# First-batch q and k rows over all partitions, halves swapped in the cast, and a block of unread products moved ahead of the first channel mix

## The chip, the cores and the metric

The kernel runs on one core of a Trainium2 chip. The metric is the device time of one execution in microseconds (us); lower is better. A core has TensorE (PE, matrix products), VectorE (DVE), ScalarE (ACT), GpSimd (POOL) and SyncE (SP), which here only issues transfers. Times of before are from three runs and one profiled execution.

## What is computed

Eight batches of 576 tokens with 8 heads of 64 channels go through block-causal attention (blocks of 64 tokens, each block sees itself and the earlier ones); the result, 512 channels per token, goes through a channel mix with a hidden width of 1024. All inputs and the output are float32 in DRAM.

```python
scores = scale * np.matmul(q, k.transpose(0, 1, 3, 2))
scores = np.where(block_i >= block_j, scores, -1000000000.0)
attn = softmax(scores)                    # over the keys
x = np.matmul(attn, v)                    # heads side by side: (B, S, 512)
x_prev = x shifted by one token, zero ahead of the first
xk = mu_k * x + (1.0 - mu_k) * x_prev
xr = mu_r * x + (1.0 - mu_r) * x_prev
k = np.maximum(xk @ w_k, 0.0)             # 512 -> 1024
v = k * k @ w_v                           # 1024 -> 512
r = 1.0 / (1.0 + np.exp(-(xr @ w_r)))     # 512 -> 512
return r * v
```

## The kernel before

**Order.** All work is registered as tasks with an engine, a planned duration, a rank, what it depends on, and the buffers it takes from rings. `Plan.order` walks a planned clock and at each moment gives each engine the ready task of lowest rank; the program is then written in that order, so every engine's queue has a fixed order and only semaphores decide the real times. The ranks stand in a table `RANK`, most of it for the first batch (`loads`, `qkt0`, `score0`, `av0`, `xt0`, `mix0`, `pk0`, `pr0`, `pv0`), and a few offsets (`qk`, `v`, `qkt`, `av`, `xt`, `mix`, `xr`, `moe`) that hold for every later batch. So a change of a rank or of a planned duration can move instructions anywhere in the program. All loads and stores are issued by SP, in one queue.

**Attention of one batch.** q and k are loaded, cast to bf16 (`t_nb`), transposed on PE by a product with an identity, and copied out of PSUM to `t_qkt` (channels on partitions). Scores (`t_s`, L509) are exponentiated on ACT to `t_e` (L530; three pieces for a pair of heads, and one further piece `EL` for the last 64 keys of all heads), POOL zeroes the masked corners (L538). Then come the products with v (`t_mm` in batch 0, `t_m` later, L567; 15 for a head, with a column of ones for the sum), a reciprocal and a multiplication on DVE (L584, L585, output `t_x`), and a transpose back (L637) that ACT copies to `t_xt` (L616). `t_e` has three buffers for four pairs of heads, `t_s` two.

**The first batch's q and k** are loaded differently from the others: a tile holds 4 heads (a group, g = 0 or 1), and each partition holds nine consecutive tokens of a head, which are 2304 contiguous bytes. The tile is [128, 2, 576] and uses the rings of `t_xk` (q) and `t_xr` (k), which the channel mix needs only later. One transfer fills 64 partitions with two heads, a second the other 64. Two casts, one for each of the tile's two columns of heads, write `t_nb`, and `add_long_qkt` transposes it in nine blocks of 128x128: eight of q, eight of k, and the ninth of both together.

**The channel mix** works on chunks of 512 tokens, nine in all. For each 128 channels, POOL or DVE subtracts the shifted tokens (`t_d`, L675), DVE makes `t_xk` and `t_xr` (L687). `add_pk` multiplies with WK (L723, 4 products of 128x512 for each of eight parts), ACT takes the relu to `t_kr` (L733) and DVE squares it (L739). `add_pr` multiplies with WR (L752) and ACT takes a tanh; `add_pv` multiplies with WV (L775) and DVE joins the two to `t_o`, which SP stores. The results of pk, pr and pv, of batch 0's products with v, and of the unread products below share two PSUM buffers (`mm`). The weights come as 20 loads into the ring `ld` of ten buffers and are cast to fp16, WK by POOL, WR and WV by ACT.

**Unread products.** `warm` multiplies an identity with itself, four products of 128x128 at a time, into an `mm` buffer that nobody reads. It depends on nothing and has the highest ranks (1000 and up), so the plan puts the 18 tasks (72 products) wherever PE has nothing else at the start: 48 before the first transposes, 12 after q's, 12 after k's.

Of the kernel before, what the change touches and what calls it, by code (L numbers as in the profile page):

```python
# [13 lines left out]
ALU = mybir.AluOpType  # L14


WARM = 18

RANK = {
# [18 lines left out]
 'qkt': -5.5,  # L40
 'av': 3.0,
 'xt': 5.5,
 'mix': 41.5,
 'xr': 114.5,
 'moe': 17.5,
}


# [90 lines left out]
def kernel(  # L139
# [13 lines left out]
    B, H, S, D = q.shape  # L153
# [17 lines left out]
    plan = Plan(RINGS)  # L171
# [10 lines left out]
    def new(ring, shape, dtype):  # L182
        return pools[ring].tile(shape, dtype, tag=ring, name="t_" + ring)
# [26 lines left out]
    def step(b, n=0):  # L210
        return b * NP_ + n

    tiles = {}


    def load(dst_key, make, jobs, rank, dur, deps=(), takes=(), uses=()):
        def fn():
            if make is not None:
                tiles[dst_key] = make()
            for dst, src in jobs(tiles[dst_key]):  # L220
                nc.sync.dma_start(dst, src)  # L221
# [34 lines left out]

    JT = S // D

    LONG = {(0, 0): ("DVE", "POOL"), (0, 1): ("POOL", "ACT"),
            (1, 0): ("POOL", "DVE"), (1, 1): ("POOL", "DVE")}  # L260

    def add_long(g, ranks):


        for n, src in enumerate((q, k)):
            ring = ("xk", "xr")[n]
            ld, nb = plan.buf(ring), plan.buf("nb")
            tiles["nbbuf", 0, g, n] = nb
            key = ("ld", 0, g, n)
            t = load(key, lambda ring=ring: new(ring, [P, 2, S], FP),  # L270
                     lambda d, src=src: [
                         (d[y * D:y * D + D], src[
                             0, 4 * g + 2 * y:4 * g + 2 * y + 2].rearrange(
                                 "x (p j) d -> p x (j d)", j=JT))
                         for y in range(2)], ranks[n], 1.8, takes=[ld])
            cast["qk", 0, g, n] = []
            for x in range(2):
                def fn(n=n, key=key, x=x):
                    if x == 0:
                        tiles["nb", 0, g, n] = new("nb", [P, JT, P], BF)  # L280
                    dst = tiles["nb", 0, g, n][:, :, x * D:x * D + D]
                    src = tiles[key][:, x].rearrange("p (j d) -> p j d", d=D)
                    eng = LONG[g, n][x]
                    if eng == "ACT":
                        nc.scalar.copy(dst, src)
                    elif eng == "DVE":
                        nc.vector.tensor_copy(dst, src)
                    else:
                        nc.gpsimd.tensor_copy(dst, src)
                cast["qk", 0, g, n].append(on(  # L290
                    LONG[g, n][x],
                    {"ACT": 0.7, "DVE": 0.5, "POOL": 0.78}[LONG[g, n][x]],
                    ranks[n], fn, [t], takes=[] if x else [nb],
                    uses=[ld] + ([nb] if x else [])))

    def add_tail(b, rank):
        tl, tb = plan.buf("tl"), plan.buf("tb")
# [55 lines left out]
    evac = {}  # L353
# [311 lines left out]
    def add_mix(c, cc, rank):  # L665
        d = plan.buf("d")
        if cc == 0:
            tiles["xkb", c], tiles["xrb", c] = plan.buf("xk"), plan.buf("xr")
            mixed[c, 0], mixed[c, 1] = [], []
        eng = "DVE" if cc % 2 else "POOL"  # L670

        def fn():
            tiles["d", c, cc] = new("d", [P, CH], FP)
            x = tiles["xt", c]
            (nc.vector if eng == "DVE" else nc.gpsimd).tensor_tensor(  # L675
                tiles["d", c, cc], x[:, cc, 1:CH + 1], x[:, cc, 0:CH],
                ALU.subtract)
        sub = on(eng, 0.8 if eng == "DVE" else 1.3, rank, fn,
                 list(xt_of[c][cc]), takes=[d], uses=[xtbuf[c]])
        for n in range(2):  # L680
            name = ("xk", "xr")[n]
            buf = tiles[name + "b", c]

            def mul(n=n, name=name):
                if cc == 0:
                    tiles[name, c] = new(name, [P, CCn, CH], F16)
                nc.vector.scalar_tensor_tensor(  # L687
                    tiles[name, c][:, cc], tiles["d", c, cc],
                    (MUK1, MUR1)[n][:, cc:cc + 1],
                    tiles["xt", c][:, cc, 1:CH + 1], ALU.mult, ALU.add)  # L690
# [116 lines left out]
    R = RANK  # L807


    wbuf = plan.buf("mm")  # L810

    def warm(i):
        if i == 0:
            tiles["warm"] = new("mm", [P, CH], FP)
        for x in range(4):
            nc.tensor.matmul(tiles["warm"][:, x * P:(x + 1) * P], identb,
                             identb, start=True, stop=True)
    for i in range(WARM):
        on("PE", 0.43, 1000 + i, lambda i=i: warm(i), [],
           takes=[] if i else [wbuf], uses=[wbuf] if i else [])  # L820

    at = {x: -99 + i for i, x in enumerate(R["loads"])}
    t = on("SP", 0.6, at["mu"], mus, [])
    mu_ready.append(on("DVE", 0.3, at["mu"], mu1, [t]))
    for b in range(B):
        r = step(b)
        if b == 0:
            for g in range(2):
                add_long(g, [at[f"g{g}q"], at[f"g{g}k"]])
# [82 lines left out]
```

## Time and profile before

| | |
|---|---|
| median of 3 runs | 294.98 us (294.54 to 295.31) |
| the profiled execution | 294.23 us, span of its instructions 292.1 us |
| PE busy | 271.1 us, 93% of the span |
| DVE, ACT, POOL busy | 76%, 64%, 46% |
| DMA | 43.44 MB; most loads have pieces of 256 bytes |
| granted PE clock, mean over the span | 0.959 |

The profile page gives busy times, 40 equal slices of the span (7.3 us each) with the busy tenths of each engine and the PE clock granted, the chain of work that ended last, and groups of instructions by line. Other views of the same trace: the chain in order of time, a timeline of instructions with the idle time ahead of each and what ended it ("[2.75 <-DMA t_xk]"), and tables of busy times in stretches that one chooses. "SPq" is SP issuing a transfer. A count ("x10") joins instructions of one kind that follow each other.

### The profile page before, as it was taken

The numbers are of one execution on the slowest core, as the hardware profiler recorded it, in microseconds if no ns is written. First come the engines' busy times: TensorE is split into PE (matmuls) and PEld (weight loads), VectorE is DVE, ScalarE is ACT, GpSimd is POOL, SyncE is SP. The second block draws the span as 40 slices with busy tenths as digits, with TensorE's granted clock in tenths as the row PEclk, the third lists the DMA queues.
The fourth block names the chain that finished last, engine by engine and source line by source line (L and its number), as shares of the span: only waits on it lengthen the run. The fifth ranks groups of instructions, "written<-read, shape, count | busy, mean of one in ns | idle before, by whom it ended". The sixth has DMA issues, their size and how long they took to land.

```text
span 292.1 us, 6893 instructions
## 1 busy us (share of the span) xinstructions
PE 271.1 (93%) x2584; PEld 154.8 (53%) x2584; DVE 221.4 (76%) x394; ACT 187.1 (64%) x295; POOL 134.8 (46%) x283
## 2 busy tenths in 40 slices
PE   7658669999799999999999999999999999999995
PEld 7425425566465545664655655565556555544442
DVE  3453896459979686998599779977986797898541
ACT  0587935867669548864886588657866795361530
POOL 2256763667868573956395618371512123301000
PEclk9676959999899999999999999999999999999999
DMA  7999999489999999939996895111001101201102
GB/s 163 260 204 322 323 202 210 121 189 218 212 198 216 212 244 209 244 78 209 274 204 130 218 237 116 38 45 66 2 36 41 73 1 39 108 0 74 72 36 108
DMA packets 114337, 43.44 MB, mean 149 GB/s; under 512 B 106112, under 2 KB 106112, under 8 KB 114304
## 3 DMA queue, kind: packets, MB, share of 16 engines
q1 hardware_dynamic: 114304, 43.01, 62.3%
q8 instruction: 20, 0.33, 0.5%
q14 instruction: 13, 0.11, 0.1%
HBM read 33.56 MB, written 9.44 MB: 147 GB/s over the span
## 4 chain that ended last, share of the span: by engine, by line
PE 82%; DVE 8%; DMA 5%; ACT 1%; SPq 1%; issue 1%; POOL 1%; DVEq 0%; POOLq 0%
PE t_mm L775 22%; PE t_mm L723 21%; PE t_mm L752 10%; PE t_m L567 9%; PE t_s L509 8%; PE t_m L637 6%; PE t_m L370 5%; DMA t_xk<-in_q_dram 2%; DMA t_xr<-in_k_dram 2%; PE t_mm L567 1%; DVE t_k L739 1%; SPq L221 1%; DVE t_xk L687 1%; DVE t_x L585 1%; DVE t_d L675 1%
## 5 line engine op out<-in xcount | busy, mean ns | idle before, releaser
L530 ACT ACTIVATE t_e<-t_s 128x1024 f16<-128x1024 f32 x96 | 95.3, 1024 | 26.7 <-PE t_s L509 23.6
L723 PE MATMUL t_mm<-t_xk,WK 128*128 128x512 f16 x288 | 72.7, 391 | 4.9 <-DVE t_xk L687 4.1
L775 PE MATMUL t_mm<-WV,t_k 128*128 128x512 f16 x288 | 66.8, 379 | 0.7 <-ACT t_t L762 0.7
L739 DVE TENSOR_TENSOR t_k<-t_kr 128x512 f16<-128x512 f32 x72 | 56.7, 797 | 10.8 <-ACT t_kr L733 10.6
L538 POOL MEMSET t_e<- 64x128 f16 x128 | 23.7, 200 | 77.6 <-ACT t_e L530 74.1
L733 ACT ACTIVATE t_kr<-t_mm 128x512 f32<-128x512 f32 x72 | 43.1, 599 | 21.2 <-PE t_mm L723 20.8
L775 PEld LDWEIGHTS <-t_k 128*128 128x128 f16 x288 | 27.5, 98 | 33.3 <-issue 2.7
L248 POOL CAST t_nb<-t_ld 128x512 bf16<-128x512 f32 x56 | 42.7, 779 | 4.0 <-DMA t_ld<-in_q_dram 1.6
L723 PEld LDWEIGHTS <-WK 128*128 128x128 f16 x288 | 27.1, 100 | 32.3 <-issue 9.0
L785 DVE SCALAR_TENSOR_TENSOR t_o<-t_t,t_mm 128x512 f32<-128x512 f32 x36 | 24.7, 685 | 20.8 <-PE t_mm L775 13.6
L567 PEld LDWEIGHTS <-t_e 128*128 128x128 f16 x896 | 34.3, 99 | 9.7 <-PE t_s L509 2.7
L509 PE MATMUL t_s<-t_qkt 64*128 64x64 bf16 (+4 forms) x384 | 34.3, 288 | 4.2 <-DVE t_qkt L446 2.2
L616 ACT COPY t_xt<-t_m 128x256 f32<-128x256 f32 (+7 forms) x68 | 24.0, 394 | 20.4 <-PE t_m L637 20.4
L752 PE MATMUL t_mm<-WR,t_xr 128*128 128x512 f16 x144 | 36.8, 382 | 0.0
L567 PE MATMUL t_m<-VO,t_e 128*128 128x65 f16 x784 | 32.9, 195 | 0.4 <-DVE t_qkt L389 0.2
L762 ACT ACTIVATE t_t<-t_mm 128x512 f32<-128x512 f32 x36 | 21.6, 600 | 17.0 <-PE t_mm L752 16.3
L687 DVE SCALAR_TENSOR_TENSOR t_xk<-t_d,MUK,t_xt 128x512 f16<-128x512 f32 x36 | 30.1, 844 | 0.3
L675 POOL TENSOR_TENSOR t_d<-t_xt 128x512 f32<-128x512 f32 x18 | 21.3, 1182 | 19.7 <-ACT t_xt L616 9.4
L687 DVE SCALAR_TENSOR_TENSOR t_xr<-t_d,MUR,t_xt 128x512 f16<-128x512 f32 x36 | 29.7, 836 | 0.0
L322 POOL CAST VO<-t_vl 128x512 f16<-128x512 f32 (+1 forms) x40 | 28.4, 728 | 2.1 <-DMA t_vl<-in_v_dram 0.9
L585 DVE TENSOR_TENSOR t_x<-t_m,t_r 128x320 f32<-128x320 f32 x56 | 27.5, 491 | 1.9
L509 PEld LDWEIGHTS <-t_qkt 64*128 64x128 bf16 x384 | 12.8, 96 | 25.5 <-issue 17.5
(54 smaller groups left out, 239.5 us busy)
## 6 DMA issues: line engine op xcount, KB each, us to landing
out_dram<-t_o SPq DMA_DIRECT2D x36, 256.0 KB, 2.1
t_vl<-in_v_dram SPq DMA_DIRECT2D x32, 256.0 KB, 5.0
t_ld<-in_q_dram SPq DMA_DIRECT2D x56, 128.0 KB, 3.6
t_ld<-in_k_dram SPq DMA_DIRECT2D x56, 128.0 KB, 3.4
t_ld<-in_moe_w_k_dram SPq DMA_DIRECT2D x8, 256.0 KB, 5.3
t_ld<-in_moe_w_v_dram SPq DMA_DIRECT2D x8, 256.0 KB, 5.8
t_xk<-in_q_dram SPq DMA_DIRECT2D x4, 288.0 KB, 5.4
t_xr<-in_k_dram SPq DMA_DIRECT2D x4, 288.0 KB, 5.6
```

The lines of the kernel that those rows point to most:

```text
L248: nc.gpsimd.tensor_copy(tiles["nb", b, pr][:, n], tiles[key][:, :].rearrange("p t h d -> p t (h d)"))
L322: nc.gpsimd.tensor_copy(VOs[b % 2][0:n, sc, :, 0:D], tiles["vl", b, sc][0:n])
L509: nc.tensor.matmul(PS[:, h, col:col + n], qkt[rows, pr, 1, kc * P:kc * P + P], qkt[rows, pr, 0, q0:q0 + n], start=True, stop=True)
L530: nc.scalar.activation(tiles["e", b, pr][:, :, i, :], tiles["ps", b, it], AF.Exp, scale=ISQ)
L567: nc.tensor.matmul(PA[:, mt * D1:(mt + 1) * D1], stationary(b, h, kc, mt), VOs[b % 2][:, kc, h, 0:D1], start=(kc == 0), stop=(kc == mt))
L585: nc.vector.tensor_tensor(tiles["x", b, pr][:, :, h % 2 * D:(h % 2 + 1) * D], view[:, :, 0:D], Rc[:, :].unsqueeze(2).to_broadcast([P, 5, D ...
L687: nc.vector.scalar_tensor_tensor(tiles[name, c][:, cc], tiles["d", c, cc], (MUK1, MUR1)[n][:, cc:cc + 1], tiles["xt", c][:, cc, 1:CH + 1], ...
L723: nc.tensor.matmul(ps, WK[:, cc, jc * P:(jc + 1) * P], tiles["xk", c][:, cc], start=(cc == 0), stop=(cc == CCn - 1))
L733: nc.scalar.activation(tiles["kr", c, jc], tiles["pk", c, jc], AF.Relu)
L739: nc.vector.tensor_tensor(tiles["k2", c][:, jc], KR, KR, ALU.mult)
L752: nc.tensor.matmul(ps, tiles["xr", c][:, cc, jt * P:(jt + 1) * P], WR[:, cc], start=(cc == 0), stop=(cc == CCn - 1))
L775: nc.tensor.matmul(ps, tiles["k2", c][:, jc, jt * P:(jt + 1) * P], WV[:, jc], start=(jc == 0), stop=(jc == JCn - 1))
```

## The change

The first batch's q and k transfers each cover all 128 partitions: the two heads of one transfer are contiguous in DRAM, and go to partitions 0-63 and 64-127 of one column of the tile. The heads therefore sit at other places than before, and the cast puts them right: of its four pieces (64 partitions x 576 elements each), two stay in their half of the partitions and two move to the other half. There are 16 casts where there were 8, distributed over DVE, ACT and POOL by the table `LONG`. The unread products are no longer free to stand at the start: they depend on the normalised results of all eight heads of batch 0 and have rank -5, there are twelve tasks (48 products) instead of 18 (72), and their planned time is lower. All ranks are new.

```diff
-WARM = 18
+WARM = 12
...
- 'loads': ['g0q', 'g0k', 'g1q', 'wk6', 'wv2', 'wv5', 'v4', 'mu', 'wv4',
...
+ 'loads': ['g0q', 'g0k', 'g1k', 'g1q', 'wk7', 'v0', 'wk2', 'v4', 'v2',
...
- 'qk': [-30.5, -24.0, -13.0, -12.5],
+ 'qk': [-17.0, -15.0, -11.5, -14.5],
...
-    LONG = {(0, 0): ("DVE", "POOL"), (0, 1): ("POOL", "ACT"),
-            (1, 0): ("POOL", "DVE"), (1, 1): ("POOL", "DVE")}
+    LONG = {(0, 0): ("DVE", "POOL", "DVE", "ACT"),
+            (0, 1): ("ACT", "POOL", "DVE", "ACT"),
+            (1, 0): ("POOL", "DVE", "DVE", "POOL"),
+            (1, 1): ("POOL", "DVE", "DVE", "POOL")}
...
-                         (d[y * D:y * D + D], src[
-                             0, 4 * g + 2 * y:4 * g + 2 * y + 2].rearrange(
-                                 "x (p j) d -> p x (j d)", j=JT))
-                         for y in range(2)], ranks[n], 1.8, takes=[ld])
+                         (d[:, x], src[0, 4 * g + 2 * x:4 * g + 2 * x + 2]
+                          .rearrange("y (p j) d -> (y p) (j d)", j=JT))
+                         for x in range(2)], ranks[n], 1.8, takes=[ld])
...
-            for x in range(2):
+            for i, (x, y) in enumerate(((0, 0), (1, 1), (1, 0), (0, 1))):
+                eng = LONG[g, n][i]
...
-                    dst = tiles["nb", 0, g, n][:, :, x * D:x * D + D]
-                    src = tiles[key][:, x].rearrange("p (j d) -> p j d", d=D)
+                    dst = tiles["nb", 0, g, n][
+                        x * D:x * D + D, :, y * D:y * D + D]
+                    src = tiles[key][y * D:y * D + D, x].rearrange(
+                        "p (j d) -> p j d", d=D)
...
-                    {"ACT": 0.7, "DVE": 0.5, "POOL": 0.78}[LONG[g, n][x]],
+                    eng, {"ACT": 0.7, "DVE": 0.5, "POOL": 0.68}[eng],
...
-    for i in range(WARM):
-        on("PE", 0.43, 1000 + i, lambda i=i: warm(i), [],
-           takes=[] if i else [wbuf], uses=[wbuf] if i else [])
...
+    wbuf = plan.buf("mm")
+    for i in range(WARM):
+        on("PE", 0.3, -5, lambda i=i: warm(i),
+           [evac["x", 0, h] for h in range(H)],
+           takes=[] if i else [wbuf], uses=[wbuf] if i else [])
```

SP's queue at the start of the program; each row is a transfer's tile, source and shape. Before:

```order
L221 DMA t_xk<-in_q_dram 64x2x576 x2
L221 DMA t_xr<-in_k_dram 64x2x576 x2
L221 DMA t_xk<-in_q_dram 64x2x576 x2
L221 DMA t_ld<-in_moe_w_k_dram 128x512
L221 DMA t_ld<-in_moe_w_v_dram 128x512 x2
L221 DMA t_vl<-in_v_dram 64x8x64
L799 DMA MUK<-in_moe_mu_k_dram 128x4x1
L800 DMA MUR<-in_moe_mu_r_dram 128x4x1
L221 DMA t_ld<-in_moe_w_v_dram 128x512
L221 DMA t_xr<-in_k_dram 64x2x576 x2
L221 DMA t_vl<-in_v_dram 128x8x64 x4
```

Now:

```order
L221 DMA t_xk<-in_q_dram 128x576 x2
L221 DMA t_xr<-in_k_dram 128x576 x4
L221 DMA t_xk<-in_q_dram 128x576 x2
L221 DMA t_ld<-in_moe_w_k_dram 128x512
L221 DMA t_vl<-in_v_dram 128x8x64
L221 DMA t_ld<-in_moe_w_k_dram 128x512
L221 DMA t_vl<-in_v_dram 64x8x64
L221 DMA t_vl<-in_v_dram 128x8x64 x2
L221 DMA t_ld<-in_moe_w_k_dram 128x512
L221 DMA t_vl<-in_v_dram 128x8x64
```

The second group's k, which stood behind three weights of WV, one of WK, a part of v and the two mu, now stands third, and the second group's q fourth; v comes between single weights.

DVE's queue from its first cast on (L444 and L446, now L450 and L452, copy transposed blocks to `t_qkt`). Before:

```order
L287 CAST t_nb<-t_xk 128x9x64
L434 MEMSET t_qkt 128x4x32
L444 COPY t_qkt<-t_m 128x2x64x8
L446 COPY t_qkt<-t_m 128x4x64
L287 CAST t_nb<-t_xk 128x9x64
L444 COPY t_qkt<-t_m 128x2x64x8
L803 TENSOR_SCALAR MUK_139<-MUK 128x4
L804 TENSOR_SCALAR MUR_140<-MUR 128x4
L287 CAST t_nb<-t_xr 128x9x64
L444 COPY t_qkt<-t_m 128x2x64x8
L446 COPY t_qkt<-t_m 128x4x64
```

Now:

```order
L294 CAST t_nb<-t_xk 64x9x64 x2
L440 MEMSET t_qkt 128x4x32
L450 COPY t_qkt<-t_m 128x2x64x8
L294 CAST t_nb<-t_xr 64x9x64 x3
L452 COPY t_qkt<-t_m 128x4x64
L294 CAST t_nb<-t_xk 64x9x64 x2
L450 COPY t_qkt<-t_m 128x2x64x8 x2
L452 COPY t_qkt<-t_m 128x4x64
```

DVE has seven casts where it had three; one cast of the first group's k stands behind the copy of q, and two of the second group's k stand ahead of the copy that the first scores need.

ACT's queue from batch 0's last exponentials to the first relu (WV and WR are casts of weights). Before:

```order
L530 ACTIVATE t_e<-t_s 128x2x512 x6
L344 CAST WR<-t_ld 128x512
L616 COPY t_xt<-t_m 128x512 x2
L347 ACTIVATE WV<-t_ld 128x512 x2
L344 CAST WR<-t_ld 128x512
L347 ACTIVATE WV<-t_ld 128x512
L616 COPY t_xt<-t_m 128x512 x2
L344 CAST WR<-t_ld 128x512 x2
L347 ACTIVATE WV<-t_ld 128x512
L616 COPY t_xt<-t_m 128x4x64
L347 ACTIVATE WV<-t_ld 128x512
L733 ACTIVATE t_kr<-t_mm 128x512 x3
```

Now:

```order
L536 ACTIVATE t_e<-t_s 128x2x512 x2
L622 COPY t_xt<-t_m 128x512 x2
L353 ACTIVATE WV<-t_ld 128x512 x4
L350 CAST WR<-t_ld 128x512
L622 COPY t_xt<-t_m 128x512
L622 COPY t_xt<-t_m 128x4x64
L353 ACTIVATE WV<-t_ld 128x512
L350 CAST WR<-t_ld 128x512 x2
L353 ACTIVATE WV<-t_ld 128x512
L350 CAST WR<-t_ld 128x512
L353 ACTIVATE WV<-t_ld 128x512
L739 ACTIVATE t_kr<-t_mm 128x512 x7
```

More of the casts of WV and WR stand behind the last copies of `t_xt`: six between the copy of 4x64 and the first relu, where there was one.

On PE the 72 unread products at the start are gone; 48 stand between the last transposes of batch 0's results (L643) and the first product with WK (L729). On DVE, `t_xk` and `t_xr` of the first 128 channels now stand ahead of the normalisation of the last two heads, not behind it. For the later batches, the new offsets let SP load a batch's q and k in one stretch and later in the order than before, when the first pair of heads was loaded up to two batches ahead.

More of the change, by code (lines that the diff above doesn't have):

```diff
@@ L14 @@
 ALU = mybir.AluOpType
-WARM = 18
+WARM = 12
 RANK = {
[18 rows of a table removed]
- 'qkt': -5.5,
[L41 to L45, printed above, removed]
[18 rows of a table added]
+ 'qkt': -5.5,
+ 'av': 3.5,
+ 'xt': 6.0,
+ 'mix': 26.0,
+ 'xr': 52.5,
+ 'moe': 18.0,
 }
@@ L271, in add_long, with fn @@
                      lambda d, src=src: [
-                         (d[y * D:y * D + D], src[
-                             0, 4 * g + 2 * y:4 * g + 2 * y + 2].rearrange(
-                                 "x (p j) d -> p x (j d)", j=JT))
-                         for y in range(2)], ranks[n], 1.8, takes=[ld])
+                         (d[:, x], src[0, 4 * g + 2 * x:4 * g + 2 * x + 2]
+                          .rearrange("y (p j) d -> (y p) (j d)", j=JT))
+                         for x in range(2)], ranks[n], 1.8, takes=[ld])
             cast["qk", 0, g, n] = []
-            for x in range(2):
-                def fn(n=n, key=key, x=x):
-                    if x == 0:
+            for i, (x, y) in enumerate(((0, 0), (1, 1), (1, 0), (0, 1))):
+                eng = LONG[g, n][i]
+                def fn(n=n, key=key, x=x, y=y, i=i, eng=eng):
+                    if i == 0:
                         tiles["nb", 0, g, n] = new("nb", [P, JT, P], BF)
-                    dst = tiles["nb", 0, g, n][:, :, x * D:x * D + D]
-                    src = tiles[key][:, x].rearrange("p (j d) -> p j d", d=D)
-                    eng = LONG[g, n][x]
+                    dst = tiles["nb", 0, g, n][
+                        x * D:x * D + D, :, y * D:y * D + D]
+                    src = tiles[key][y * D:y * D + D, x].rearrange(
+                        "p (j d) -> p j d", d=D)
                     if eng == "ACT":
@@ L290, in add_long @@
                 cast["qk", 0, g, n].append(on(
-                    LONG[g, n][x],
-                    {"ACT": 0.7, "DVE": 0.5, "POOL": 0.78}[LONG[g, n][x]],
-                    ranks[n], fn, [t], takes=[] if x else [nb],
-                    uses=[ld] + ([nb] if x else [])))
+                    eng, {"ACT": 0.7, "DVE": 0.5, "POOL": 0.68}[eng],
+                    ranks[n], fn, [t], takes=[] if i else [nb],
+                    uses=[ld] + ([nb] if i else [])))
     def add_tail(b, rank):
@@ L807 @@
     R = RANK
-    wbuf = plan.buf("mm")
     def warm(i):
```

32 rows, old and new, of the table RANK are left out of this document.

## The prediction

> **What bounds the kernel now.** I read the page's busy times and slices first, then a table of stretches, then the chain in order of time for the start. In the stretch rows the columns are PE, PE's weight loads, DVE, ACT and POOL busy, the granted PE clock, DMA share and GB/s.
>
> ```profile
> span 292.1 us, 6893 instructions
> PE 271.1 (93%) x2584; PEld 154.8 (53%) x2584; DVE 221.4 (76%) x394; ACT 187.1 (64%) x295; POOL 134.8 (46%) x283
> ```
>
> ```profile
> 27.00:29.00 2.00, 2.00 (x40) 1.51 (x39) 1.19 (x5) 1.97 (x3) 1.49 (x4) 0.97 1.05 399
> 30.00:40.00 10.00, 4.76 (x55) 3.08 (x51) 9.71 (x17) 7.11 (x14) 7.50 (x10) 0.87 1.05 266
> 70.00:80.00 10.00, 7.76 (x91) 4.78 (x90) 9.68 (x18) 7.60 (x13) 8.86 (x19) 0.92 1.10 213
> 100.00:150.00 50.00, 49.28 (x504) 28.26 (x502) 39.93 (x74) 35.88 (x59) 30.56 (x62) 1.00 0.91 205
> ```
>
> From about 40 us on PE is the bound (49.28 of 50 us busy), except between 70 and 80, where DVE is (9.68 of 10). Before 40 us PE waits, and in the last ten of these DVE carries the work (9.71). So a microsecond saved ahead of the first dense stretch of products is worth a microsecond at the end, as long as 70 to 80 doesn't take it back. The chain shows what the start consists of:
>
> ```profile
> 4.13 7.22 DMA t_xk<-in_q_dram
> 12.01 6.03 DMA t_xr<-in_k_dram
> 18.13 0.77 DVE t_nb L287
> ...
> 22.47 0.59 ACT EL L518
> ...
> 24.63 1.76 PE t_mm L567 x30
> ...
> 39.33 4.42 PE t_mm L723 x10
> 43.75 1.14 PE t_mm L752 x4
> 44.88 1.73 PE t_mm L723 x8
> ```
>
> Two loads of the second group in a row lead to its cast at 18.13; dense work begins at 39.33, its first ten products at 442 ns, the later eight at 216.
>
> **The loads.** The start in order of time (start, length, engine, line, what ended the idle time before):
>
> ```profile
> 0.75 1.39 SPq L221 DMA_DIRECT2D t_xk<-in_q_dram  x2
> 6.05 0.75 DVE L287 CAST t_nb<-t_xk 128x576 bf16<-128x576 f32 x1 [2.75 <-DMA t_xk<-in_q_dram]
> 6.08 0.66 POOL L289 CAST t_nb<-t_xk 128x576 bf16<-128x576 f32 x1 [4.25 <-DMA t_xk<-in_q_dram]
> 7.59 1.23 DVE L444 COPY t_qkt<-t_m 128x1024 bf16<-128x1024 bf16 x1 [0.65 <-PE t_m L421]
> 8.74 1.28 ACT L285 ACT_TABLE_LOAD   x1 [8.74 <-DMA t_xr<-in_k_dram]
> 10.03 0.67 ACT L285 CAST t_nb<-t_xr 128x576 bf16<-128x576 f32 x1
> 10.85 1.23 PE L421 MATMUL t_m<-identb,t_nb 128*128 128x128 bf16 x10 [2.62 <-ACT t_nb L285]
> 12.11 1.29 DVE L446 COPY t_qkt<-t_m 128x256 bf16<-128x256 bf16 x1 [3.29 <-PE t_m L421]
> 13.04 0.95 DVE L287 CAST t_nb<-t_xk 128x576 bf16<-128x576 f32 x1
> 14.20 1.94 ACT L530 ACTIVATE t_e<-t_s 128x1024 f16<-128x1024 f32 x2 [0.76 <-PE t_s L509]
> 20.82 1.26 DVE L446 COPY t_qkt<-t_m 128x256 bf16<-128x256 bf16 x1
> ```
>
> q is in at 6.05 and k at 8.74: 1.35 us for a transfer of 288 KB, 219 GB/s. Counted back, data begin to land at 3.35. The trace has no such row for 128 partitions. The bounds are 1.35 (no gain) and 0.74 (the 399 GB/s of 27 to 29 us, where weights of 128 rows of 2 KB arrive). I take 0.80, near the second, since the shape is almost that one. SP needs 0.70 for an issue, so it stays ahead. Then q's two transfers land at 4.15 and 4.95, k at 6.55, the second k at 8.15, the second q at 9.75.
>
> **The casts.** Sixteen for eight, and 64 partitions instead of 128 shorten nothing if the time goes by the 576 elements of a partition: I keep 0.75 on DVE, 0.66 on POOL, 0.67 on ACT. The ends are half of these and, for a cast that moves between halves or runs beside POOL's, DVE's slower one of 0.95. ACT's table load, which here waits for k, stands in the new order ahead of all waits and is hidden by the wait for q; with that cover gone it costs 1.28. q: DVE 4.15 to 4.90 and 4.95 to 5.70, POOL to 5.61, ACT to 4.82; eight transposes at 123 ns (the ten in 1.23) to 6.7; DVE's copy to 8.0; DVE's piece of k to 8.75; ten transposes to 10.0. Meanwhile two DVE casts of the second k, to 10.25, then the copy that the first scores need, 1.29: 11.55. Before, that copy ended at 13.40 and ACT began 0.80 later, so the first exponential moves from 14.20 to 12.35: 1.85 earlier. The second group: two casts (1.5), three copies (1.23, 1.23, 1.26), 16.8, against 22.08. Five exponentials at 0.97 from 12.35 last to 17.2, so ACT no longer waits for the second group.
>
> **To the last normalisation.**
>
> ```profile
> 27.03 2.85 ACT L530 ACTIVATE t_e<-t_s 128x1024 f16<-128x1024 f32 x3 [1.25 <-POOL t_e L538]
> 29.05 0.59 PE L567 MATMUL t_mm<-VO,t_e 128*128 128x65 f16 x14
> 32.08 0.49 DVE L585 TENSOR_TENSOR t_x<-t_mm,t_r 128x320 f32<-128x320 f32 x1
> 32.18 0.99 SPq L221 DMA_DIRECT2D t_ld<-in_moe_w_v_dram  x1
> 34.33 1.09 DVE L687 SCALAR_TENSOR_TENSOR t_xr<-t_d,MUR,t_xt 128x512 f16<-128x512 f32 x1
> 36.79 0.68 DVE L675 TENSOR_TENSOR t_d<-t_xt 128x512 f32<-128x512 f32 x1
> 37.51 1.77 DVE L687 SCALAR_TENSOR_TENSOR t_xk<-t_d,MUK,t_xt 128x512 f16<-128x512 f32 x2
> 38.11 0.63 ACT L347 ACTIVATE WV<-t_ld 128x512 f16<-128x512 f32 x1 [1.23 <-DMA t_ld<-in_moe_w_v_dram]
> ```
>
> New ACT order from 17.2: one exponential, EL 0.59, three more, one weight 0.63: 22.2. The last three need the first pair's buffer, and so its products with v: behind the sixth exponential (18.2) POOL has a weight and the last part of v, 0.66 each, to 19.6; PE can begin when the score ahead in its queue has its buffer, about 20.1, and is done about 21.9 (1.76, as before). With a copy to `t_xt` and a wait for PE between them, the last exponential ends about 26.9 instead of 29.88, 3.0 earlier. Two products with v at 0.6, and the last heads leave PE about 28.9. But DVE now has `t_xk` and `t_xr` of the first channels (1.09 each) ahead of the last two normalisations; it ends at about 31.2 instead of 32.57. That order also takes two of the multiplications from behind them: what is left until the last `t_xk` is two subtractions (0.8 and 0.7) and three multiplications (0.9 to 1.1): 4.6 instead of 6.7. Dense work can start at 31.2 + 4.6 = 35.8; I put 36.0, against 39.33. Ends: 34 (shorter casts and multiplications) and 38 (slow loads, POOL beside DVE).
>
> **The 48 products and the clock.**
>
> ```profile
> 1.37 5.30 PE L816 MATMUL t_mm<-identb 128*128 128x128 bf16 x48 [1.37 <-POOL identb masks.py:199]
> 7.39 0.83 PE L816 MATMUL t_mm<-identb 128*128 128x128 bf16 x12
> ```
>
> ```profile
> 39.30:41.00 1.70, 1.68 (x5) 0.57 (x5) 1.70 (x3) 0.60 (x1) 1.01 (x2) 0.50 1.02 226
> 43.00:44.00 1.00, 1.00 (x4) 0.33 (x3) 1.00 (x2) 0.21 (x1) 0.77 (x2) 0.50 0.87 181
> ```
>
> Here the dense stretch runs at half the clock until 44. The block in front of it costs 48 x 69 ns = 3.3 us at full clock, 48 x 110 = 5.3 cold. It stands behind the last transposes, about 32.5, and ends at 35.8 in the good case: hidden by DVE's multiplications. Removing the 72 at the start saves nothing, since PE waits for loads there; the colder transposes are priced above. At 44.88 this kernel has done 16 products of 512 columns; warm, they take 16 x 216 ns = 3.46, so the changed kernel is there at 39.5. That is 5.4 earlier: 3.3 from the start of dense work, less 0.4 for the two of the 16 that this kernel has done before 39.33, and 2.5 from the clock (the other 14 take 5.55 now, 3.02 warm).
>
> The Trainium skill's page "TensorE: Matmul & The Clock Gate" (Part 1) gives a budget of about 3.4 us of half clock in place of the 4.7 that the rows show. By that estimate the clock would be worth 1.7, not 2.5, and the kernel would come out 0.8 later; the rows differ from the page here, and the sum goes by the rows.
>
> **What waits next.** After the block, relu stands behind six casts of weights on ACT: the last copy to `t_xt` ends about 33.1 (32.5 and 0.6), and 33.1 + 6 x 0.63 = 36.9, while the first pk ends at 36.9 and PE has two buffers; the first square waits for DVE's `t_xr`. I take 0.4 for both (0 to 2.5). The weights' last loads wait for free buffers, which POOL and ACT casts give back about 30 to 31; with 5.9 us to land (the last one here was issued at 32.18 and cast at 38.11) they would be there at 37.
>
> The later batches' new order I price at 0, since PE has no idle to lose there, with 2 either way for 70 to 80, where it has 2.2 idle and a clock of 0.92.
>
> **Sum.** 5.4 - 0.4 = 5.0 us. The profiled execution took 294.23 (span 292.1 and 2.1 around it), so 289.2; it lies 0.75 under the median of 294.98, by which the forecast is 290.0.
>
> **Rivals.** (1) The block doesn't warm PE. For: only transposes and a wait lie ahead of it, about 3 us behind the last products with v, and at 39.33 the clock was down after two waits of 2 us with one product between. Against: the eight heads' products run close together up to there. It then costs 5.3 - 3.3 = 2.0 at most, and the 2.5 as well if it stays cold: 292 to 294.5. Part 4 of the same page of the Trainium skill says that transposes do not count as activity for the clock gate, which speaks for this rival; no run here shows it. (2) The gain is given back at 70 to 80: if the second chunk's mix isn't earlier, PE waits there 5 us more, 294 to 295. For: DVE 9.68 of 10. Against: dense work from 39 on is all PE's own, so the second batch's attention moves with it, and q, k and v of the first batches now come in the order of use. (3) Slower: later batches get q and k later. The offset -30.5 becomes -17; if a batch's transposes then wait for their casts, PE loses it seven times. It decides from 5.0 / 7 = 0.7 us a batch on; with 1.2 a batch the time is 290 + 7 x 1.2 = 298.4. For: DMA share near 1 until 100, so loads cannot hurry. Against: offsets of -17 and -5.5 are 11.5 of 13 steps apart, nearly a batch of some 28 us (253 us from 39 on for nine chunks), for loads that land in under 6. (4) The wider loads are no faster: casts then start as before, 1.35 a transfer, and by the same walk the copy for the first scores ends at 14.2 in place of 11.55; 2.65 later gives 292.6. For: the trace has no row of this shape. Against: the weights' 399 GB/s.
>
> **Numbers.** Forecast 0.60, (1) 0.12, (2) 0.10, (3) 0.10, (4) 0.08. The forecast's own range is 287 to 292.5 (2 earlier by the end of 34, 2.5 later by the relu). To leave out no more than 2 in 10 the whole reaches from 286.5 to 295. Under 0.3%, 0.9 us, this measurement can't tell a change: faster 0.80, same 0.08, slower 0.12.
>
> **What would show it.** Right: the first casts near 5 us, the second group's under 11, the first exponential near 12.4, the last normalisation near 31, the 48 products ending within half a microsecond of the first L729, that one near 36 at 216 ns each with a clock of 1.00, and 80 to 250 as before. Wrong: products of 440 ns behind the block, ACT's relu waiting for a weight, a wider gap at 65 to 80, or waits of PE for `t_nb` in every batch.

## The result, and the profile after

The changed kernel takes 287.69 us (median of four runs, 287.47 to 288.56) against 294.89 (294.54 to 295.31) beside it: a ratio of 0.9761, 95% interval 0.9737 to 0.9785. Measured again on another chip it took 288.27 (287.13 to 289.22) against 294.67, 0.9799 (0.9757 to 0.984). The first profiled execution took 287.58, span 285.8, so 6.3 less span than before. Forecast were 290.0 in 286.5 to 295. The direction, the place and the sum up to 45 us were right, the sum in part because two errors cancel. Of the 2.3 us beyond the forecast, 1.3 are in the profiled span: 0.2 up to 45 us and 1.1 behind it, in a part that I had priced at nothing. Another 0.35 lie around the span (2.13 us before, 1.78 now), and the rest is where the two profiled executions lie among their runs.

The start after, rows picked from the timeline (start, length, engine, line, what ended the idle time before):

```profile
0.75 0.86 SPq L221 DMA_DIRECT2D t_xk<-in_q_dram  x2
3.69 0.67 ACT L292 CAST t_nb<-t_xk 64x576 bf16<-64x576 f32 x1 [1.66 <-DMA t_xk<-in_q_dram]
3.69 1.52 DVE L294 CAST t_nb<-t_xk 64x576 bf16<-64x576 f32 x2 [0.40 <-DMA t_xk<-in_q_dram]
4.49 0.66 POOL L296 CAST t_nb<-t_xk 64x576 bf16<-64x576 f32 x1 [2.67 <-DMA t_xk<-in_q_dram]
5.94 1.35 ACT L292 CAST t_nb<-t_xr 64x576 bf16<-64x576 f32 x2 [1.58 <-DMA t_xr<-in_k_dram]
9.98 1.29 DVE L452 COPY t_qkt<-t_m 128x256 bf16<-128x256 bf16 x1
11.31 1.51 DVE L294 CAST t_nb<-t_xk 64x576 bf16<-64x576 f32 x2
12.07 1.02 ACT L536 ACTIVATE t_e<-t_s 128x1024 f16<-128x1024 f32 x1 [1.45 <-PE t_s L515]
15.69 1.28 DVE L452 COPY t_qkt<-t_m 128x256 bf16<-128x256 bf16 x1
...
26.38 1.97 ACT L536 ACTIVATE t_e<-t_s 128x1024 f16<-128x1024 f32 x2
```

q lands at 3.69 and 4.49, k at 5.94. A cast of 64 partitions takes 0.75 on DVE like one of 128 before, whether it stays in its half or moves. The first exponential is 2.1 earlier (14.20 before), the last ends at 28.35 instead of 29.88.

From the last normalisation to the dense products:

```profile
30.83 0.49 DVE L591 TENSOR_TENSOR t_x<-t_mm,t_r 128x320 f32<-128x320 f32 x1
...
32.07 2.00 DVE L693 SCALAR_TENSOR_TENSOR t_xk<-t_d,MUK,t_xt 128x512 f16<-128x512 f32 x2
32.37 2.84 PE L820 MATMUL t_mm<-identb 128*128 128x128 bf16 x48
34.70 0.75 DVE L693 SCALAR_TENSOR_TENSOR t_xk<-t_d,MUK,t_xt 128x512 f16<-128x512 f32 x1
35.05 1.89 PE L729 MATMUL t_mm<-t_xk,WK 128*128 128x512 f16 x8
35.50 0.63 ACT L353 ACTIVATE WV<-t_ld 128x512 f16<-128x512 f32 x1 [0.48 <-DMA t_ld<-in_moe_w_v_dram]
...
36.82 0.63 ACT L353 ACTIVATE WV<-t_ld 128x512 f16<-128x512 f32 x1
37.36 1.07 ACT L739 ACTIVATE t_kr<-t_mm 128x512 f32<-128x512 f32 x2
37.99 3.61 PE L729 MATMUL t_mm<-t_xk,WK 128*128 128x512 f16 x16 [1.05 <-ACT t_kr L739]
```

The last normalisation ends at 31.32. The 48 products take 59 ns each and end as the last `t_xk` comes; dense products start at 35.05, 216 ns each (16 take 1.72 more than 8). After eight of them PE waits 1.05 for a relu that stands on ACT behind casts of weights. The sixteenth is done at 37.99 + 8 x 0.216 = 39.7, against 44.88.

Stretches (PE, weight loads, DVE, ACT, POOL busy, granted clock, DMA share, GB/s), first of after, then of before. A stretch or a product is called cold where PE has half its clock; a product of 512 columns then takes 442 ns instead of 216.

```profile
20.00:27.00 7.00, 6.58 (x91) 5.03 (x92) 2.62 (x11) 4.96 (x7) 3.14 (x10) 0.56 1.04 366
39.00:45.00 6.00, 5.91 (x47) 3.17 (x44) 5.41 (x10) 3.58 (x6) 4.27 (x5) 1.00 1.03 221
78.00:82.00 4.00, 4.00 (x39) 2.05 (x37) 2.28 (x4) 4.00 (x8) 2.85 (x7) 1.00 1.24 225
```

```profile
20.00:32.00 12.00, 9.31 (x156) 6.70 (x156) 6.77 (x18) 9.23 (x14) 7.36 (x19) 0.72 0.98 316
36.00:44.00 8.00, 5.05 (x13) 1.75 (x13) 7.96 (x10) 2.92 (x6) 4.99 (x7) 0.58 0.98 203
78.00:82.00 4.00, 3.73 (x36) 2.44 (x36) 3.63 (x7) 1.72 (x3) 3.13 (x9) 0.57 1.10 228
```

Before had a second stretch at half clock, at 78 to 82, behind the wait for the second chunk's `t_xk`; after has none. Between 65 and 80 the changed kernel waits as well, longest here:

```profile
71.27 1.06 PE L643 MATMUL t_m<-identf,t_x 128*128 128x128 f32 x8 [1.64 <-DVE t_x L591]
74.99 1.89 PE L729 MATMUL t_mm<-t_xk,WK 128*128 128x512 f16 x8 [0.47 <-POOL t_xk L708]
```

The second chunk's first product comes at 74.99 (78.27 before). All waits of PE over 0.15 us from 40 us on add up to 2.8 us after and 2.9 before.

### The profile page after: what moved, and what is told of

It reads as the page before. It is cut to its first block, busy times and chain, and to the rows that moved or that the text cites. A ratio compares the mean times of both kernels' runs of the same rounds, so it can differ in the third digit from the quotient of the medians.

```text
span 285.8 us, 6843 instructions
## 1 busy us (share of the span) xinstructions
PE 264.8 (93%) x2560; PEld 151.0 (53%) x2560; DVE 221.3 (77%) x398; ACT 188.3 (66%) x297; POOL 134.3 (47%) x285
## 4 chain that ended last, share of the span: by engine, by line
PE 83%; DVE 6%; ACT 5%; DMA 3%; POOL 1%; issue 1%; SPq 0%; POOLq 0%; DVEq 0%
PE t_mm L781 21%; PE t_mm L729 20%; PE t_mm L758 11%; PE t_s L515 9%; PE t_m L573 8%; PE t_m L643 6%; PE t_m L376 5%; ACT t_e L536 2%; DMA t_ld<-in_q_dram 2%; PE t_mm L573 2%; DVE t_nb L294 1%; ACT t_xt L622 1%; PE t_m L427 1%; DMA t_xk<-in_q_dram 1%; DVE t_xk L693 1%
## 5 line engine op out<-in xcount | busy, mean ns | idle before, releaser
L729 PE MATMUL t_mm<-t_xk,WK 128*128 128x512 f16 x288 | 69.6, 379 | 1.7 <-ACT t_kr L739 1.1
L248 POOL CAST t_nb<-t_ld 128x512 bf16<-128x512 f32 x56 | 41.1, 744 | 7.7 <-DMA t_ld<-in_q_dram 2.5
L729 PEld LDWEIGHTS <-WK 128*128 128x128 f16 x288 | 26.1, 98 | 28.0 <-issue 4.3
L573 PE MATMUL t_m<-VO,t_e 128*128 128x65 f16 x784 | 32.0, 193 | 0.0
L693 DVE SCALAR_TENSOR_TENSOR t_xk<-t_d,MUK,t_xt 128x512 f16<-128x512 f32 x36 | 29.0, 813 | 1.3 <-POOL t_d L681 0.8
L643 PE MATMUL t_m<-identf,t_x 128*128 128x128 f32 x160 | 24.8, 281 | 3.0 <-DVE t_x L591 3.0
## 6 DMA issues: line engine op xcount, KB each, us to landing
t_xk<-in_q_dram SPq DMA_DIRECT2D x4, 288.0 KB, 4.4
t_xr<-in_k_dram SPq DMA_DIRECT2D x4, 288.0 KB, 4.9
```

The lines of the kernel that those rows point to most:

```text
L248: nc.gpsimd.tensor_copy(tiles["nb", b, pr][:, n], tiles[key][:, :].rearrange("p t h d -> p t (h d)"))
L573: nc.tensor.matmul(PA[:, mt * D1:(mt + 1) * D1], stationary(b, h, kc, mt), VOs[b % 2][:, kc, h, 0:D1], start=(kc == 0), stop=(kc == mt))
L643: nc.tensor.matmul(px[:, i * P:(i + 1) * P], src, identf, is_transpose=True, start=(i == 0), stop=(i == 3))
L693: nc.vector.scalar_tensor_tensor(tiles[name, c][:, cc], tiles["d", c, cc], (MUK1, MUR1)[n][:, cc:cc + 1], tiles["xt", c][:, cc, 1:CH + 1], ...
L729: nc.tensor.matmul(ps, WK[:, cc, jc * P:(jc + 1) * P], tiles["xk", c][:, cc], start=(cc == 0), stop=(cc == CCn - 1))
```

## The experiments

Twelve kernels ran, each timed beside the kernel before on its own chip; their rows have line numbers of their own, a few higher or lower. "Gain" is the kernel before's median less the kernel's.

| kernel | us | ratio to before (95%) | gain |
|---|---|---|---|
| the changed kernel, again | 288.27 | 0.9799 (0.9757 to 0.984) | 6.4 |
| changed, narrow loads | 289.60 | 0.9824 (0.9792 to 0.9857) | 5.2 |
| changed, no block | 289.64 | 0.9836 (0.9805 to 0.9867) | 5.1 |
| changed, all old offsets | 296.58 | 1.0062 (1.0039 to 1.0086) | -1.8 |
| changed, old mix and xr | 288.57 | 0.9792 (0.9747 to 0.9837) | 6.3 |
| before, new offsets | 292.10 | 0.9911 (0.9872 to 0.9949) | 2.6 |
| before, block ahead of the mix | 291.72 | 0.9891 (0.9854 to 0.9927) | 3.1 |
| before, products at 73 to 78 | 293.74 | 0.9961 (0.9933 to 0.9988) | 1.0 |
| changed, casts moved | 287.67 | 0.9772 (0.973 to 0.9814) | 7.0 |
| the same, and products at 16 to 20 | 288.30 | 0.9799 (0.9759 to 0.9839) | 6.4 |
| the same, one cast put back | 286.91 | 0.9731 (0.9696 to 0.9765) | 7.9 |
| the same, no block | 286.43 | 0.9730 (0.9685 to 0.9776) | 8.4 |

**The changed kernel again.**

> The changed kernel itself, beside the other three on one chip, so that its own spread between runs is known: 287.4 to 288.6 us. If the runs without the block and with the narrow loads (289.6 each on another chip) lost nothing and only that chip was slower, this one comes near 289.5 as well.

288.27: the other chip cost at most about 0.6. The ten runs of this kernel on the two chips lie at 287.1 to 289.2, median 288.0; the next two are held against that. Both lose 1.6 us by it. Their ratios lie above the interval of the first measurement and overlap with that of the second, so the loss is likely, not certain. In the profile of the changed kernel again, the slowest of its six runs:

```profile
36.79 0.63 ACT L353 ACTIVATE WV<-t_ld 128x512 f16<-128x512 f32 x1 [1.10 <-DMA t_ld<-in_moe_w_v_dram]
39.27 3.10 PE L729 MATMUL t_mm<-t_xk,WK 128*128 128x512 f16 x13 [1.66 <-ACT t_kr L739]
```

ACT's late weight came at 36.79 instead of 35.50, PE waited 1.66 for the relu, and the span was 287.4. But the dense products had already begun 0.7 later (35.73 for 35.05): both the start and the landing of these weights vary between executions.

**Undo the wide loads.**

```diff
-(d[:, x], src[0, 4*g + 2*x:4*g + 2*x + 2].rearrange("y (p j) d -> (y p) (j d)", j=JT))
+(d[x*D:x*D + D], src[0, 4*g + 2*x:4*g + 2*x + 2].rearrange("y (p j) d -> p y (j d)", j=JT))
...
-src = tiles[key][y * D:y * D + D, x]
+src = tiles[key][x * D:x * D + D, y]
```

> The changed kernel in the same order, with the four q and k loads written to 64 partitions a transfer as before; each cast then reads the half it writes. Theory A (the wider loads carry the earlier start): 1.35 us a transfer instead of 0.8, so the second q transfer is in at 6.0 instead of 4.5, k at 8.7 instead of 5.9, the first exponential at 14 instead of 12.07; the start of the dense products moves by 1.5 to 2.6 us: 289.2 to 290.3 us. Rival B (the casts and copies set the start, the shape of the load is hidden): under 288.2.

289.6 is in theory A's range. In its timeline:

```profile
4.58 0.67 ACT L293 CAST t_nb<-t_xk 64x576 bf16<-64x576 f32 x1 [2.56 <-DMA t_xk<-in_q_dram]
5.87 0.75 DVE L295 CAST t_nb<-t_xk 64x576 bf16<-64x576 f32 x1 [0.55 <-DMA t_xk<-in_q_dram]
14.58 1.02 ACT L537 ACTIVATE t_e<-t_s 128x1024 f16<-128x1024 f32 x1 [2.55 <-PE t_s L516]
39.07 3.18 PE L730 MATMUL t_mm<-t_xk,WK 128*128 128x512 f16 x14 [0.47 <-ACT t_kr L740]
```

The pace is back at 1.29 a transfer (4.58, 5.87) and the first exponential at 14.58. These 2.5 us shrink on the way: the dense products begin 1.7 later than in the first profile of the changed kernel (36.71 for 35.05), and PE's restart behind the relu is 1.1 later (39.07 for 37.99); there ACT waits 0.48 for a weight ahead of the relu, here it does not. The profiled execution is the fastest of its five runs: its span is 1.0 longer, the median of the five spans 1.6 (287.8 against 286.2 over the ten runs of the changed kernel).

**Undo the block.**

```diff
 def warm(i):
-    for x in range(4): nc.tensor.matmul(...)
+    pass
```

> The changed kernel in the same order, without the 48 unread products. Theory A (the block keeps the clock up): the first products of the channel mix run at 440 ns and a granted clock of 0.50 for about 4.7 us; 2.3 lost, of which the 1.05 us wait for relu at 37 hides a part: 288.9 to 290.0 us. Rival B (the clock is at 1.00 ahead of the block at 32.4 and stays there, so the block is worth nothing): 287.4 to 288.0, products of 216 ns.

```profile
36.45 1.24 PE L729 MATMUL t_mm<-t_xk,WK 128*128 128x512 f16 x5 [1.01 <-DVE t_xk L693]
39.54 3.61 PE L729 MATMUL t_mm<-t_xk,WK 128*128 128x512 f16 x16 [1.85 <-ACT t_kr L739]
```

```profile
36.00:44.00 8.00, 5.70 (x35) 2.91 (x35) 6.58 (x11) 5.24 (x9) 3.67 (x5) 1.00 1.01 220
```

289.64 is inside theory A's range, but its mechanism is not in the profiled execution: the products take 216 ns over waits of 1.01 and 1.85. Their time is the sign to go by, because the clock column misses a stretch in this trace. It reads 1.00 from 20 to 27, where fourteen products with v take 0.95 us, as they do in the first profile at a clock of 0.56; at full clock they take 0.58:

```profile
20.00:27.00 7.00, 6.34 (x76) 4.51 (x74) 2.22 (x9) 4.85 (x6) 3.34 (x10) 1.00 0.99 353
21.73 0.95 PE L573 MATMUL t_mm<-VO,t_e 128*128 128x65 f16 x14
```

Beside the profile of the changed kernel again, whose weights were as late, nothing is lost: PE restarts at 39.54 and 39.27, the spans are 287.5 and 287.4. So the median and the profiled execution don't agree, and the 1.6 us stay unexplained. There is one hint for the block: three of the six runs without it have a mean clock of 0.970 to 0.976, and none of the ten with it is under 0.982. But two of these three are no slower than the rest (spans of 287.0 and 287.3). The last pair of kernels below tries the block again.

**The later batches' offsets**, three kernels. First the changed kernel with the old ones:

```diff
- 'qk': [-17.0, -15.0, -11.5, -14.5], 'v': -11.0, 'av': 3.5, 'xt': 6.0, 'mix': 26.0, 'xr': 52.5, 'moe': 18.0
+ 'qk': [-30.5, -24.0, -13.0, -12.5], 'v': -13.0, 'av': 3.0, 'xt': 5.5, 'mix': 41.5, 'xr': 114.5, 'moe': 17.5
```

> The changed kernel with the offsets of the later batches (qk, v, av, xt, mix, xr, moe) of the kernel before; the first 40 us stay as they are. Theory A (the new offsets took away the second stretch of half clock at 78 to 82): it comes back a few us earlier, 440 ns products, 289.0 to 289.8 us. Rival B (it went away because the start is earlier, or by the wait's length alone): the time of the changed kernel, 287.4 to 288.2.

296.58: with the old offsets the new start is worth less than nothing. Both theories were far too small. Its profiled execution lay 3.6 above the median, so it gives no more than a hint on the place: PE's longer waits from 39 us on add up to 11.2 us there, 4.7 for the relu, 2.4 for `t_x`, 2.1 for a cast of v, and only 0.3 for `t_nb`. Then the reverse, the kernel before with the new offsets:

> The kernel before (narrow loads, block at the start) with the offsets of the later batches of the changed kernel. With the old offsets the new start gave 296.6, with the new ones 287.7, so this fills the fourth place. Theory A (the new offsets are better by themselves, the old ones cost PE its waits from 66 to 125 us): faster than before, 289 to 293.5 us, with the cold first products still there. Rival B (start and offsets only fit each other in pairs; a planner's order for one start is bad for another): slower than before, 296 to 302 us.

```profile
36.00:44.00 8.00, 5.24 (x13) 1.87 (x13) 7.35 (x10) 3.15 (x7) 4.35 (x6) 0.58 1.13 217
78.00:82.00 4.00, 3.95 (x40) 1.98 (x37) 3.81 (x9) 3.66 (x6) 3.17 (x9) 1.00 1.06 231
```

292.1, theory A: the first cold stretch is as before, the second is gone. But rival B's thought holds as well. The new start alone gains -1.8, the new offsets alone 2.6, and both together 6.4: 5.6 us come only with the pair. And the changed kernel with two of the seven old:

```diff
- 'mix': 26.0, 'xr': 52.5
+ 'mix': 41.5, 'xr': 114.5
```

> The changed kernel with two of the offsets of the kernel before alone: mix 41.5 for 26, xr 114.5 for 52.5. All seven together gave 296.6. Theory A (subtractions and multiplications put off by 15 to 60 steps come too late for the earlier start): most of the loss, 293 to 297 us. Rival B (it is qk, -30.5 for -17 and on, whose early loads and casts take buffers and POOL's time): within 1 us of the changed kernel, 287.5 to 289.

288.57, theory B as far as it says that it is not these two. Which of `qk`, `v`, `av`, `xt` and `moe` it is was not tried.

**The clock of the kernel before**, two kernels: eight unread products at each of three waits between 73 and 78, and 72 ahead of the first channel mix.

```diff
+for task in (PE's 6th and 2nd task ahead of pk(1, 0), and pk(1, 0)):   # ahead of each
+    for x in range(8): nc.tensor.matmul(more[...], identb, identb, start=True, stop=True)
```

> The kernel before, with three times 8 unread products ahead of the transposes at 73.3, the transposes at 75.9 and the first product of the second channel mix at 78.3, where PE waits 0.36, 0.47 and 0.79 us. Theory A (the second cold stretch costs 1.7 us and comes from about 5.5 us in which PE has only transposes, scores and waits): products of 216 ns from 78.3 on, 293.0 to 293.6 us. Rival B (the clock falls there whatever PE does, or the blocks' 1.4 us stand in the way): 294.9 to 296.3.

```profile
40.75 4.43 PE L724 MATMUL t_mm<-t_xk,WK 128*128 128x512 f16 x10 [2.67 <-DVE t_xk L687]
```

```profile
78.00:82.00 4.00, 3.59 (x51) 2.29 (x51) 3.96 (x6) 3.29 (x6) 3.34 (x7) 1.00 1.07 232
```

The first cold stretch stays (ten products in 4.43), the second goes; 1.0 us is gained where 1.2 to 1.9 were expected, the interval (0.4 to 2.0) holds both. The other:

```diff
+if t is first:        # the first task of pk
+    for x in range(72): nc.tensor.matmul(more[...], identb, identb, start=True, stop=True)
```

> The kernel before with 72 unread products added ahead of the first product of the channel mix (34.5 us), where PE waits 2.03 us twice for t_xk. Theory A (the block alone keeps the clock; the 14 products of 442 ns take 216): 2.0 to 2.5 us faster than before, 292.2 to 292.8. Rival B (the block runs at half the clock, 7.9 us, and ends behind the last t_xk at 39.3): 1 to 3 us slower than before, 295.7 to 297.7.

```profile
35.63 4.18 PE L888 MATMUL t_mm<-identb 128*128 128x128 bf16 x72
40.86 2.32 PE L724 MATMUL t_mm<-t_xk,WK 128*128 128x512 f16 x10 [0.61 <-DVE t_xk L687]
```

```profile
36.00:44.00 8.00, 7.21 (x84) 5.01 (x81) 7.96 (x10) 3.83 (x8) 6.05 (x6) 1.00 0.93 216
78.00:82.00 4.00, 3.88 (x54) 2.34 (x53) 3.93 (x8) 2.64 (x4) 3.13 (x7) 1.00 0.95 213
```

291.72, more than theory A expected. Ten products that took 4.42 take 2.32, and the stretch at 78 is at full clock too, though nothing was put there and the wait ahead of it is still 0.77 us.

**The relu and the cold attention**, four kernels. First POOL casts two parts of WK earlier and three of WR, and three loads of weights are moved ahead; this frees buffers for the last loads and takes casts from ACT's queue:

```diff
+elif name == "r" and i in (0, 2, 3): nc.gpsimd.tensor_copy(WR[:, i], w)
+for w in (("k", 4), ("r", 2), ("k", 3)):            # the loads of these parts
+    ahead_of(cast["w", w[0], w[1]]["deps"][0], subs[0, 0])
+ahead_of(cast["w", "k", 4], subs[0, 0])            # POOL's first subtraction
+ahead_of(cast["w", "k", 3], ready["z", 0, 3, 2, 0])  # memset of the last exponential
```

> The changed kernel with two of POOL's casts of WK ahead of the subtraction at 26.6 and behind it, so that SP's next weight is sent at about 26 instead of 31.5, and with three of ACT's casts of WR on POOL. Theory A (relu waits behind ACT's casts, and these for late weights, which costs PE 1.05 us at 36.9 and more in runs where the weights land later): no wait for t_kr, 286.4 to 287.0 us where the changed kernel beside it has 287.7. Rival B (the wait has a cover: PE then waits for wk5's cast or for t_nb instead): within 0.4 us of the changed kernel.

```profile
32.92 1.47 PE L645 MATMUL t_m<-identf,t_x 128*128 128x128 f32 x8 [2.08 <-DVE t_x L593]
34.18 4.12 PE L824 MATMUL t_mm<-identb 128*128 128x128 bf16 x48
38.14 4.05 PE L733 MATMUL t_mm<-t_xk,WK 128*128 128x512 f16 x18
```

The relu wait is gone, and 0.6 is gained, less than runs of one kernel differ by and less than theory A asked for. The profiled execution is the slowest of seven (289.9). In it the first of the two casts, at 26.90, waits 1.65 for its weight with the subtraction and the memsets behind it, and DVE's `t_xr` takes 1.60 instead of 0.75 beside POOL. The last normalisation ends at 32.77 instead of 31.32, PE waits 2.08, the clock falls and the block takes 86 ns a product. Next, with unread products between the scores:

```diff
+if t is one of the last five scores ahead of the first products with v:
+    for x in range(6): nc.tensor.matmul(more[...], identb, identb, start=True, stop=True)
```

> The kernel of e6 with six unread products ahead of each of the five last scores before the first products with v (16 to 20.5 us), where PE waits 0.25 to 0.6 us for exponentials and its clock falls to 0.50 at 20. Theory A (the clock then stays at 1.00, three heads' products with v take 1.2 instead of 1.76 us a pair, the last exponential ends at 27 to 27.8 instead of 28.35, the dense products start 0.5 to 1.2 us earlier): 285.5 to 286.5 us. Rival B (transposes, scores and such products do not keep the clock up, or the exponentials alone set the pace): the time of e6 within 0.3 us.

```profile
20.00:27.00 7.00, 6.66 (x125) 4.97 (x122) 4.09 (x15) 6.82 (x9) 3.00 (x10) 1.00 0.99 356
```

```profile
24.37 1.95 ACT L541 ACTIVATE t_e<-t_s 128x1024 f16<-128x1024 f32 x2
26.85 0.61 POOL L348 CAST WK<-t_ld 128x512 f16<-128x512 f32 x1 [2.67 <-DMA t_ld<-in_moe_w_k_dram]
28.78 0.27 PE L578 MATMUL t_mm<-VO,t_e 128*128 128x65 f16 x3 [1.44 <-POOL t_e L549]
```

The step expected is there: full clock (fourteen products with v take 0.59), and the last exponential ends at 26.32, 2.0 earlier. Nothing of it reaches the end, since POOL's cast waits 2.67 for a weight with the memsets behind it. So one cast and the three loads were put back, and the other cast was only moved ahead of the second subtraction:

```diff
-for w in (("k", 4), ("r", 2), ("k", 3)): ahead_of(cast["w", w[0], w[1]]["deps"][0], subs[0, 0])
-ahead_of(cast["w", "k", 4], subs[0, 0]); ahead_of(cast["w", "k", 3], ready["z", 0, 3, 2, 0])
+ahead_of(cast["w", "k", 4], subs[0, 2])
```

> The changed kernel with the thirty unread products among the scores at 16 to 20.5 us, three casts of WR on POOL, and one cast of WK ahead of POOL's second subtraction only (so none stands in front of the memsets of the last exponentials). Theory A (the start is bound by POOL's memsets and ACT's queue; with both free the exponentials end at 26.3 as in e7, the last normalisation at 29, the dense products start at about 33.3 and run without the wait for t_kr): 1.7 plus 1.0 earlier than the changed kernel, 284.8 to 286.2 us. Rival B (an earlier start is given back between 65 and 80, where PE then waits longer for t_x and t_xk): 287.3 us or more.

```profile
33.24 0.81 PE L736 MATMUL t_mm<-t_xk,WK 128*128 128x512 f16 x3
34.37 3.83 PE L736 MATMUL t_mm<-t_xk,WK 128*128 128x512 f16 x17 [0.32 <-DVE t_xk L700]
```

286.91, the first kernel that looks faster than the changed one (median 288.0 over ten runs), by 1.1, though the intervals of the ratios overlap. The sixteenth product is done at 34.37 + 13 x 0.216 = 37.2, 2.5 earlier than in the changed kernel; 1.6 of it arrives in the span (284.2 for 285.8; this execution is the fastest of six), 1.1 in the median, between A and B. And without the block:

> The kernel of e8 without the 48 unread products ahead of the channel mix; there no wait for relu hides a slow start. Theory A (the block is worth the clock): the first products at 440 ns for 3.4 to 4.7 us, 1.7 to 2.4 us slower than e8. Rival B (PE keeps the full clock over waits of about 1 us, the block is worth nothing): within 0.5 us of e8, products of 216 ns behind the waits.

```profile
35.19 3.83 PE L736 MATMUL t_mm<-t_xk,WK 128*128 128x512 f16 x17 [1.65 <-DVE t_xk L700]
```

286.43, theory B: 17 products in 3.83 behind a wait of 1.65, at full clock. Here the block is worth nothing in the median and in the profile; one run of the six without it took 289.3 at a mean clock of 0.982, the other five 286.0 to 286.8.

## Why the prediction was right, and where it was not

**Loads.** The pace of 0.80 a transfer was right (3.69, 4.49). q was 0.46 earlier and k 0.6 earlier than forecast, which fits that an issue takes 0.43 instead of 0.70 (0.86 for two, 1.39 before); I had not used that. With the narrow loads the first cast comes at 4.58. Undoing the loads alone cost 2.5 at the first exponential and 1.6 in the median.

**Casts, first exponential.** 0.75, 0.66 and 0.67 as taken; the copy for the first scores ends at 11.27 (forecast 11.55), the first exponential starts at 12.07 (12.35). That the second group's casts end under 11 was wrong, 12.8, without effect: its copies end at 16.97, forecast 16.8.

**Last exponential.** Mis-sized: 28.35, forecast 26.9. The first pair's products with v began at 20.96 instead of 20.1, which is 0.9 of it. The rest: PE is at half clock there, as it was before (a clock of 0.72 from 20 to 32), and I carried the cold 1.76 for the first pair over without seeing that all later ones up to 26 are cold too. With products in the waits it ended at 26.32. The last normalisation was still right, 31.32 for 31.2, because there DVE has `t_xr` ahead of the last two normalisations anyway.

**Start of dense work.** 35.05, forecast 36.0: the last multiplication took 0.75, with POOL idle beside it, not 0.9 to 1.1; the two ahead of it took 1.0. The block took 2.84 and was hidden, as forecast.

**The clock, 2.5 us.** The size was right: first products at 216 ns and a clock of 1.00. The cause in the prediction, the block, is not shown for this kernel. Without it the products of the profiled execution take 216 ns as well. The new order leaves PE waits of 0.36, 0.64 and 1.01 us between the first products where the old one left 2.03 twice, which fits, but no run tested it alone. In the kernel before, with those long waits, the block takes 2.1 us off ten products; the median gain of 3.1 also holds the cold stretch at 78, which went with it. Whether the block gives the changed kernel some of the 1.6 us is open.

On this, the Trainium skill's page "TensorE: Matmul & The Clock Gate" (Part 1) says that a free-running window of about 3.4 us decides the clock. The rows agree: where a microsecond has a clock of 0.67, 0.66 of it ran at half, so in before the clock falls at 37.34 and 78.30 and is back at 44.18 and 81.72, after 6.84 and 3.42 us, two windows and one.

```profile
37.00:38.00 1.00, 0.30 (x1) 0.02 (x1) 0.96 (x2) 0.00 (x0) 0.33 (x1) 0.67 0.98 180
44.00:45.00 1.00, 1.00 (x6) 0.48 (x5) 0.79 (x2) 0.46 (x2) 0.68 (x1) 0.91 0.93 197
78.00:79.00 1.00, 0.73 (x2) 0.25 (x2) 1.00 (x3) 1.00 (x2) 1.00 (x3) 0.65 1.03 230
81.00:82.00 1.00, 1.00 (x17) 0.83 (x15) 0.86 (x3) 0.00 (x0) 0.88 (x4) 0.64 1.18 219
```

By it the 4.7 us that I put against the page's budget were only the part of two windows in which PE had work. It also fits that the same wait at 78 cools PE in one kernel and not in another, which is an argument, not a test. The two falls, 37.34 and 78.30, are 40.96 us apart, twelve times 3.41. Rival (1), the cold block, did not happen here; with casts moved and a wait of 2.08 shortly ahead of it, it did (86 ns a product instead of 59).

**Relu.** Mis-sized: 1.05 and 1.66 in two profiles, forecast 0.4. ACT's casts ended at 37.45, forecast 36.9, and 0.48 of that is the wait for a weight. The larger part of the miss is that the products had begun 0.95 earlier than forecast and so came to the wait sooner.

**Sum up to 45 us.** The sixteenth product was forecast at 39.5 and 0.4 for the waits behind, and is done at 39.7: 5.2 gained, forecast 5.0. That this is so near is partly luck: dense work that began 0.95 early pays for a relu that took 0.65 more.

**Later batches priced at 0: the step that failed.** The offsets alone gain 2.6 on the kernel before. On the new start they decide everything: 296.6 with the old ones, 288.0 with the new, 8.6. Rival (2), the gain given back later, is what happens without them, and by more than its 294 to 295; the place is only hinted at. Rival (3), waits for `t_nb` in each batch, did not come. Why the old offsets cost so much more on the new start is open. In the profiles, the second cold stretch gone is worth 3.4 x 0.5 = 1.7, which with the 5.2 gives 6.9 where the spans differ by 6.3; the waits from 40 on are equal, and 0.6 the other way I could not assign.

**Rival (4)** fell with the landing times.

## What to carry to other kernels

Before a start is made shorter, look at which queue holds the next thing that the bound engine needs: with the narrow loads, 2.5 us at the first exponential became 1.1 behind the relu and 1.6 at the end, because casts and landings of weights had their own schedule. Ranks tuned for one start can turn the gain of another into a loss, so a "steady state" part of a change is not priced at 0 because its engine looks full; its clock belongs to the price. Unread products paid where PE waited 2 us between single products. Where the order had already closed those gaps they paid nothing in one kernel (286.43 without, 286.91 with them), and in the changed kernel it is open.

## What the runs showed of the hardware

Half clock came in stretches of 3.4 us or a multiple of it: 3.42 and 6.84 in before, and 17.1 in the kernel before with the block ahead of the mix (from 11.68, by a clock of 0.84 in the microsecond from 11, to 28.76, by 0.62 in the one from 28). Waits of up to 1.85 us between products left them at 216 ns; 2.03 twice with one product between, and 2.08 behind products with v, did not. At 78 to 82 of the kernel before no single wait was over 0.79, and yet the clock fell. The clock column of a trace can miss a stretch: it reads 1.00 from 20 to 27 in the profiles of the changed kernel again, without the block and with casts moved, where fourteen products with v take 0.95 as at half clock. A transfer's issue cost SP 0.43 us for 128 partitions of 2304 bytes and 0.70 for 64 partitions of twice as much.
